# Wide early loads for the second mixture's weights, and two moves in TensorE's order

## The chip, the cores and the metric

One NeuronCore of a Trainium2 chip runs the whole program; the other cores are idle. The metric is the device time of one execution in microseconds (us), the median of a few runs. Engines are called as in the profile: PE (TensorE), PEld (its weight loads), DVE (VectorE), ACT (ScalarE), POOL (GpSimd), SP (SyncE). POOL issues the loads from memory, SP issues transposing transfers and small copies.

## The reference

Causal attention by blocks, then two mixtures that follow each other on the same tokens. All weights arrive as 64-bit floats; the tolerance lets the kernel compute with split 16-bit operands (a high and a low part, three products for one).

```python
# attention: 4 batches x 8 heads, 576 positions, 64 per head, causal by blocks of 64
scores = scale * np.matmul(q, k.transpose(0, 1, 3, 2))
scores = np.where(block_i >= block_j, scores, -1000000000.0)
attn = softmax(scores)
x = (attn @ v) laid out as 2304 tokens x 512
# first mixture
a = x @ w1            # 512 x 1024
b = x @ w2
y = (a * b @ w3) @ w_out      # 1024 x 1024, 1024 x 512
# second mixture
h = y @ w_in          # 512 x 2048
r = np.maximum(h, 0.0)
out = (r * r) @ w_out         # 2048 x 512
```

## The kernel before, in words

**Stages.** Attention runs as 16 pairs of heads (four per batch), each in three groups of rows: scores `s` on PE (L839), the largest value on DVE (L881), the exponential on ACT (L898), the probabilities `p` on ACT and DVE (L939, L946), then SP transposes `p` through a transfer (`pt`, L956) and PE multiplies it by `v` (`pv_bank`, L1031). The first mixture runs along with it, one batch behind: for each batch (576 tokens, cut into parts of 320 and 256) come the products `ab` with w1 and w2 over eight blocks f, `a` and `g` on ACT and DVE (L1277, L1284, L261), then `y` with w3 and w_out, which were multiplied together at the start (`w3o`), and the eviction `ys` on ACT (L1327) to memory. Attention is over near 375 us of the span; the first mixture's last batch and the preparation of the second mixture fill the time to some 480 us; from then to the end PE does the second mixture in blocks of 512 tokens (the first is 256). It forms `h` by a Winograd scheme with seven half-size products (`p`, L1901: operands b11, b21, t2, t3, t4, t1, b22, banks p17, p26, p45, p3), squares it, and multiplies by w_out (`p` L2069 with Strassen's scheme from the third block on, `o` L2196 before).

**Weights.** The second mixture's weights `wb` are 16 tiles of 128 x 1024 64-bit words (1 MB each), w_in in the one half of the columns and w_out in the other. `convert_pair(j)` takes tiles j and j + 8. Each half of a tile comes through `convert` (L310 to L366): a load of 128 x 512 words (512 KB) issued by POOL into one of four places `raw` (L334), two passes on ACT over the words (L342, L346), a shift and an add on DVE (L352, L355) into a place `cx`. After that the pair's norms are taken (squares on ACT L1626, L1663; small products on PE into `nq`), and ACT writes the scaled 16-bit parts `wb` (L301), DVE the low parts. Pairs 4 to 7 are kept in the four places w8_0 to w8_3 (`PAIR_HOMES`), which held w_out's words at the start of the program and are not used between the first mixture's preparation and pair 4.

**Order.** A planner (`Order`) writes every engine's instruction order. Each operation has an engine, a cost in us, the data it reads and writes, a key (rank) and a `spare`. The planner simulates the engines, and whichever engine is free next takes the lowest key among those operations whose inputs are ready by its own count; `spare` lets it count an operation's inputs as ready only that many us later, so that on PE other work comes ahead of it. An `after` entry such as ("pt", n, 2) is an order for the planner, that the operation is placed when group 2 of pair n has been transposed; it is not a wait on the chip. On the chip an engine runs its list in order and waits by semaphores for the data alone.

Of the kernel before, what the change touches and what calls it, by code (L numbers as in the profile page):

```python
# [7 lines left out]
F32 = mybir.dt.float32  # L8
# [3 lines left out]
I32 = mybir.dt.int32  # L12
# [7 lines left out]
P = 128  # L20
# [167 lines left out]
def fused_kernel(ctx: ExitStack, tc: tile.TileContext, qT, kT, vp, va, w12, w3t, wo, wb, out):  # L188
# [460 lines left out]
    def v_scales(b):  # L649
# [34 lines left out]

        key = (b * H - VSB) * HEAD
        mb_ = pv_bank[0]
        od.op(PE, 0.3, lambda: pe.matmul(mb_()[:, :P], ones(), d(), start=True, stop=True), [(ones,), (d,)], [(mb_, "pv")], key)
        e = at_buf("ve", 1, [P, H], F32, f"ve_{b}")
        t = at_buf("vsc", 2, [P, H], F32, f"vsc_{b}")
        back = at_buf("vback", 2, [P, H // 2], F32, f"vback_{b}")  # L690
# [419 lines left out]
    CHUNK = 6  # L1110
    n_unit = [0]

    def accumulate(acc, mms, n, key, c_one=c_mm, chunk=CHUNK):


        for c0 in range(0, len(mms), chunk):
            part = list(enumerate(mms))[c0 : c0 + chunk]

            def go(part=part):
                for k, (f, _) in part:  # L1120
                    l, r = f()
                    pe.matmul(acc(), l, r, start=k == 0, stop=k == len(mms) - 1)  # L1122

            keys = list(dict.fromkeys(k for _, (_, ks) in part for k in ks))
            od.op(PE, len(part) * c_one(n), go, keys, acc.keys, key)

    n_bank3 = [0]

# [24 lines left out]
    def next_key(first=K_UNIT):  # L1153
        n_unit[0] += 1
        return first + n_unit[0]
# [150 lines left out]
    def y_products(b, g, gs):  # L1306
        gt0, gn = GS[g]

        def ys_products(key=None):
            for e in range(KDM):  # L1310
                acc = Acc(gn, f"y_{b}_{g}_{e}")
                mms = []
                for f in range(KFF):
                    for a, c in PRODS:
                        mms.append((
                            lambda f=f, a=a, c=c, e=e: (w3o_view(f, a)[:, e * P : (e + 1) * P], gs[f][0][c]()),
                            [(*w3o_key(f, a), e // 2), gs[f][1][c]],
                        ))
                accumulate(acc, mms, gn, key or next_key())
                yb = buf("w2" if key else "xp", "ys", 2, [P, gn if key else GMAX], F32, f"ys_{b}_{g}_{e}")  # L1320

                def ys(yb=yb):
                    return yb()[:, :gn]

                t0 = b * S + gt0
                od.op(
                    ACT, c_act(gn), lambda acc=acc, ys=ys: act.activation(ys(), acc(), AF.Copy),  # L1327
                    [acc.key], [(yb,)], K_EVICT,
                )
                od.op(  # L1330
                    GQ, c_dma(160), lambda ys=ys, e=e, t0=t0: pool.dma_start(out=ydram[e, :, t0 : t0 + gn], in_=ys()),
                    [(yb,)], [("y", b, g, e)], K_EVICT,
                )

        if (b, g) == (B - 1, 1):
            last_y.append(ys_products)
        else:
            ys_products()
# [14 lines left out]
    KP = KFF2 // 2  # L1353
    SOON = KP // 2
    PAIR_HOMES = (0, 1, 2, 3)
    STORED_HOMES = (6, 8, 9)
    LAST = len(BLOCKS) - 1
    FIRST_S = 2
# [24 lines left out]
    def second_block():  # L1383
# [220 lines left out]
        def convert_pair(j, key):  # L1604
            if j < SOON:
                w = late(f"wbx_{j}", [P, 2, 2, 1024], f"wb_{j}", F16, 1, "wp")
            else:
                w = buf("base", f"w8_{PAIR_HOMES[j - SOON]}", 1, [P, 2, 2, 1024], F16, f"wb_{j}")
            wpair.append(w)
            home = ("wp", "cw", 4)  # L1610
            halves = {}
            for half in range(2):
                for k in range(2):
                    halves[half, k] = convert(
                        wb[j + KP * k][:, 512 * half : 512 * half + 512], None, None, None, key,
                        after=[("pt", 2 * GATE_B, 2)], home=home,
                    )
            nq, first = norms[j // SOON], SOON * (j // SOON)
            o = 2 * (j - first)
            sums = late("rs", [P, 2], f"rs_{j}", F32, 2, "wp")  # L1620
            for k in range(2):
                x, kx = halves[0, k]
                sq = buf("cv", "cx", 2, [P, 512], BF16, f"wsq_{j}_{k}")
                od.op(
                    ACT, c_act(512, 0.1),
                    lambda x=x, k=k, sq=sq: act.activation(  # L1626
                        sq(), x(), AF.Square, accum_out=sums()[:, k : k + 1]
                    ),
                    [kx], [(sq,), (sums, k)], key,
                )  # L1630

                def columns(sq=sq, k=k):
                    for kc in range(KDM):
                        pe.matmul(
                            nq()[:, o + k : o + k + 1], sq()[:, kc * P : (kc + 1) * P], ones16()[:, :1],
                            start=kc == 0, stop=kc == KDM - 1,
                        )

                od.op(PE, 0.32, columns, [(sq,), (ones16,)], [(nq, j, k)], K_NORM, S_SPARE)

            def total():
                for k in range(2):
                    pe.matmul(
                        nq()[:, 16 + o : 17 + o], ones16(), upper(sums, k, 1), start=k == 0, stop=k == 1
                    )

            od.op(PE, 0.06, total, [(ones16,), (sums, 0), (sums, 1)], [(nq, j, 2)], K_NORM, S_SPARE)
            sig = late("sig", [P, 1], f"sig_{j}", F32, 2, "wp")
            od.op(DVE, c_dve(8), lambda: shifted(th()[:, j : j + 1], nq()[:, 16 + o : 17 + o], 24), [(nq, j, 2)], [(th, j)], key)
            od.op(DVE, c_dve(8), lambda: bits(sig(), th()[:, j : j + 1], -1.0, 203.0), [(th, j)], [(sig,)], key)  # L1650
            for k in range(2):
                x, kx = halves[0, k]
                split_scaled(
                    lambda k=k: w()[:, k, 0, :512], lambda k=k: w()[:, k, 1, :512], x, 512,
                    ([(w, k, "h", 0)], [(w, k, "l", 0)], [kx]), (sig, [(sig,)]), key,
                )
            rm = late("rm", [P, 2], f"rm_{j}", F32, 2, "wp")
            for k in range(2):
                x, kx = halves[1, k]
                sq = buf("cv", "cx", 2, [P, 512], BF16, f"osq_{j}_{k}")  # L1660
                od.op(
                    ACT, c_act(512, 0.1),
                    lambda x=x, k=k, sq=sq: act.activation(  # L1663
                        sq(), x(), AF.Square, accum_out=rm()[:, k : k + 1]
                    ),
                    [kx], [(sq,), (rm, k)], key,
                )
            d = late("rd", [P, 2], f"rd_{j}", F32, 2, "wp")
            od.op(DVE, c_dve(8), lambda: shifted(rq()[:, j], rm(), 25), [(rm, 0), (rm, 1)], [(rq, j)], key)
            od.op(DVE, c_dve(8), lambda: bits(d(), rq()[:, j], -2.0, 201.0), [(rq, j)], [(d,)], key)  # L1670
            for k in range(2):
                x, kx = halves[1, k]
                split_scaled(
                    lambda k=k: w()[:, k, 0, 512:], lambda k=k: w()[:, k, 1, 512:], x, 512,
                    ([(w, k, "h", 1)], [(w, k, "l", 1)], [kx]), (lambda k=k: d()[:, k : k + 1], [(d,)]), key,
                )
# [200 lines left out]
        def h_winograd(c, j, key):  # L1877
# [12 lines left out]
            def s_of(n):  # L1890
                o, ks = sum_parts(n, j)
                return lambda a, kc: o(a)[:, kc * P : (kc + 1) * P], ks

            def product(acc, half, left, yname, spare=0.3):
                lhs, ks = left
                y = ys_[c, yname]
                mms = [(a, yn, kc) for kc in range(2) for a, yn in PRODS]

                def go():
                    for n, (a, yn, kc) in enumerate(mms):  # L1900
                        pe.matmul(  # L1901
                            acc()[:, TH * half : TH * half + TH], lhs(a, kc), y[yn]()[:, kc],
                            start=n == 0, stop=n == len(mms) - 1,
                        )

                od.op(PE, len(mms) * c_mm16(TH), go, ks + [key_of(t) for t in y], [(acc, half)], key, spare * strassen)
# [32 lines left out]
            )  # L1939
            product(b26, 0, w_of(0, 1), "b21")  # L1940
            product(b26, 1, s_of(2), "t2")
            product(b17, 1, s_of(3), "t3")
            if strassen:
                add(TH, half_of(c1, 1), half_of(b26, 1), x1, [(b26, 1), (x1,)], ck[1:])
# [2 lines left out]
            add(TH, u3, half_of(b17, 1), half_of(c1, 1), [(b17, 1), ck[1]], [(u3,)])  # L1947
            if strassen:
                add(TH, half_of(c1, 0), half_of(b26, 0), x1, [(b26, 0), (x1,)], ck[:1])
            product(b45, 0, w_of(1, 1), "t4")  # L1950
            product(b45, 1, w_of(1, 0), "t1")
            add(512, two(c2), two(b45), twice(u3), [(b45, 0), (b45, 1), (u3,)], [(c2, 0), (c2, 1)])
            add(TH, half_of(c1, 1), half_of(b45, 1), half_of(c1, 1), [(b45, 1)], [ck[1]])
# [423 lines left out]
```

## Time and profile before

| | |
|---|---|
| median of three runs | 843.76 us (842.68 to 844.37) |
| the profiled execution's own time | 844.38 us |
| its span on the page | 842.6 us (1.8 us lie around it) |
| PE busy | 822.2 us, 98% of the span |
| PEld, DVE, ACT busy | 658.6, 703.2, 606.1 us (78, 83, 72%) |
| POOL busy | 101.9 us (12%) |

The busy times say that PE is nearly always at work, and that what can be saved without removing products lies in its pauses. Matmuls overlap, so that a row's duration is longer than what it costs: one product of 256 columns in 16 bits is shown with 0.27 us but the next starts 0.11 us later, one of 320 columns 0.14 us later (a y product, 32-bit, about 0.15 us). A pause is read from starts: the distance between two successive instructions less the usual one. The idle time in square brackets behind a row is counted from the end of the row before, which is up to 0.17 us less than the pause.

### The profile page before, as it was taken

How to read it: one execution, taken by the hardware profiler on the slowest of the kernel's cores; microseconds unless marked ns; L12 is line 12 of the kernel's file. 1: busy time of each engine (PE TensorE's matmuls, PEld its weight loads, DVE VectorE, ACT ScalarE, POOL GpSimd, SP SyncE). 2: the span in 40 equal slices, each digit the busy share in tenths (PEclk: the TensorE clock that was granted, in tenths of full speed). 3: DMA queues.
4: the chain of work that ended last, by engine and by line, in shares of the span. 5: the costliest groups of instructions: out<-in, count | busy, mean ns of one | idle time of the engine just before them, and what ended most of it. 6: DMA issues, size and time to landing. Idle time of an engine off the chain costs nothing.

```text
span 842.6 us, 18679 instructions
## 1 busy us (share of the span) xinstructions
PE 822.2 (98%) x7185; PEld 658.6 (78%) x7185; DVE 703.2 (83%) x1638; ACT 606.1 (72%) x1388; POOL 101.9 (12%) x190
## 2 busy tenths in 40 slices
PE   8999999999999999999999999999999999999997
PEld 6456767778778887788879877666678888888887
DVE  6997999897778877855787889999989899787775
ACT  6997889977676777765999987565676655673552
POOL 5111211112111111011313101010020000001000
PEclk9999999999999999999999999999999999999999
DMA  8943649679998898673556422120030001001001
GB/s 325 343 147 95 195 140 213 145 167 214 203 176 171 172 180 182 145 130 104 192 179 227 140 58 69 37 90 1 2 126 1 2 7 71 1 2 51 2 1 51
DMA packets 104570, 100.18 MB, mean 119 GB/s; under 512 B 82784, under 2 KB 86624, under 8 KB 103072
## 3 DMA queue, kind: packets, MB, share of 16 engines
q0 software_dynamic: 17888, 71.18, 26.0%
q1 hardware_dynamic: 86592, 27.80, 18.5%
q8 instruction: 56, 0.92, 0.5%
q14 instruction: 34, 0.28, 0.1%
HBM read 62.78 MB, written 9.44 MB: 86 GB/s over the span
## 4 chain that ended last, share of the span: by engine, by line
PE 26%; DVE 16%; ACT 9%; issue 3%; DMA 2%; POOL 0%; DVEq 0%; ACTq 0%; POOLq 0%
PE p L1901 7%; PE p L2069 7%; PE ab L1122 6%; PE o L2196 3%; DVE c L1933 3%; ACT c L1964 2%; DMA raw<-in_wb 2%; DVE t L2024 2%; ACT c L1967 2%; PE y L1122 1%; DVE c L1975 1%; DVE gs L294 1%; DVE s L1844 1%; DVE s L1975 1%; DVE u L1933 1%
## 5 line engine op out<-in xcount | busy, mean ns | idle before, releaser
L1122 PEld LDWEIGHTS <-w 128*128 128x128 f16 x1536 | 146.9, 98 | 43.8 <-issue 6.5
L898 ACT ACTIVATE pf<-s,nm 128x192 f32<-128x192 f32 (+4 forms) x160 | 82.8, 529 | 45.2 <-DVE nm L881 44.7
L1122 PE MATMUL y<-g,w3o 128*128 128x320 f32 (+1 forms) x768 | 109.9, 299 | 1.6 <-DVE a L1284 0.8
L1122 PE MATMUL ab<-x0h,w 128*128 128x320 f16 x512 | 109.7, 299 | 0.9 <-ACT ys L1327 0.9
L1122 PEld LDWEIGHTS y<-g,w3o 128*128 128x128 f32 x768 | 103.3, 188 | 5.1 <-issue 1.2
L1122 PE MATMUL ab<-x1h,w 128*128 128x256 f16 x512 | 88.8, 273 | 0.8 <-ACT ys L1327 0.5
L2069 PEld LDWEIGHTS <-gs 128*128 128x128 f16 x816 | 79.7, 98 | 9.4 <-DVE gs L294 0.2
L1901 PEld LDWEIGHTS <-wb 128*128 128x128 f16 x768 | 75.1, 98 | 13.2 <-issue 1.2
L1122 PE MATMUL ab<-x0l,w 128*128 128x320 f16 x256 | 76.5, 299 | 0.0
L946 DVE SCALAR_TENSOR_TENSOR p<-pf,r,p 128x192 f16<-128x192 f32 (+2 forms) x120 | 62.3, 546 | 16.4 <-ACT p L939 15.8
L1122 PE MATMUL ab<-x1l,w 128*128 128x256 f16 x256 | 69.8, 272 | 0.0
L2196 PE MATMUL o<-wb,g 128*128 128x512 f16 x288 | 67.1, 379 | 0.0
L939 ACT ACTIVATE p<-pf,r 128x192 f16<-128x192 f32 (+2 forms) x120 | 61.2, 558 | 6.6 <-issue 2.6
L1901 PEld LDWEIGHTS <-st 128*128 128x128 f16 x576 | 56.1, 98 | 9.3 <-issue 2.2
L2069 PE MATMUL p<-ts,gs 128*128 128x256 f16 x480 | 61.1, 273 | 0.0
L1964 ACT ACTIVATE c<-c,beta 128x512 f32<-128x512 f32 x48 | 34.3, 715 | 35.3 <-DVE c L1933 35.1
L839 PE MATMUL s<-kraw,qraw 64*128 64x288 f32 (+4 forms) x384 | 54.0, 408 | 0.1
L2196 PEld LDWEIGHTS <-g 128*128 128x128 f16 x288 | 28.0, 98 | 28.9 <-issue 0.4
L839 PEld LDWEIGHTS s<-kraw,qraw 64*128 64x128 f32 x384 | 33.9, 186 | 15.0 <-issue 8.5
L292 ACT ACTIVATE gs<-c 128x512 f16<-128x512 f32 (+1 forms) x56 | 30.0, 536 | 21.1 <-DVE c L1975 20.9
L2069 PE MATMUL p<-wb,gs 128*128 128x256 f16 x336 | 44.5, 273 | 0.0
L873 DVE TENSOR_REDUCE nm<-s 128x2 f32<-128x384 f32 (+1 forms) x64 | 42.2, 686 | 1.0
(268 smaller groups left out, 1943.9 us busy)
## 6 DMA issues: line engine op xcount, KB each, us to landing
raw<-in_wb POOLq DMA_DIRECT2D x32, 512.0 KB, 4.9
raw<-in_w3t POOLq DMA_DIRECT2D x8, 1024.0 KB, 10.1
raw<-in_w POOLq DMA_DIRECT2D x16, 512.0 KB, 4.6
yraw<-ydram POOLq DMA_DIRECT2D x12, 512.0 KB, 4.6
vraw<-in_vp POOLq DMA_DIRECT2D x16, 320.0 KB, 4.7
qraw<-in_qT POOLq DMA_DIRECT2D x16, 288.0 KB, 4.3
kraw<-in_kT POOLq DMA_DIRECT2D x16, 288.0 KB, 4.9
vmix<-v SPq DMA_DIRECT2D x24, 160.0 KB, 4.5
```

What stands on the lines that cost most here:

```text
L292: od.op(ACT, c_act(n), lambda: act.activation(hi(), src(), AF.Copy), ks, kh, key)
L839: pe.matmul(o[:, h] if t == 4 else o, q()[rows, q_start(t) : q_start(t) + 128], keys_()[rows, c], start=True, stop=True,)
L873: lambda k=k, t=t, nm=nm, banks=banks: dve.tensor_reduce(out=nm()[:, k], in_=banks[0]()[:, :, S_COL[t] : S_COL[t] + n_keys(t)], op=ALU.max ...
L898: act.activation(o, view(a, t), AF.Exp, bias=nm()[:, k, a : a + 1], scale=SCALE, accum_out=ssum()[:, k, a : a + 1],)
L939: lambda o=o, nk=nk, a=a, k=k, w=weights, p16=p16, r=r: act.activation(p16()[:, o : o + nk], w(a, k), AF.Copy, scale=r()[:, k, a : a + 1]),
L946: lambda o=o, nk=nk, a=a, k=k, w=weights, p16=p16, r=r: dve.scalar_tensor_tensor(out=p16()[:, o + nk : o + 2 * nk], in0=w(a, k), scalar=r( ...
L1122: pe.matmul(acc(), l, r, start=k == 0, stop=k == len(mms) - 1)
L1901: pe.matmul(acc()[:, TH * half : TH * half + TH], lhs(a, kc), y[yn]()[:, kc], start=n == 0, stop=n == len(mms) - 1,)
L1933: DVE, c_dve(n), lambda: dve.tensor_tensor(out=o(), in0=x(), in1=y(), op=ALU.add), r, w, K_OUT
L1964: lambda src=src, k=k: act.activation(src(), src(), AF.Relu, scale=beta()[:, j, k : k + 1]),
L2069: pe.matmul(acc()[:, TH * u : TH * u + TH], t()[:, o : o + P], r(b), start=first and n == 0 and u == tiles[0], stop=last and n == 2 and u ...
L2196: pe.matmul(o(), g[gx]()[:, cols], wt(f)[:, a, 512:1024], start=(begin and n == 0), stop=(last and n == 2),)
```

## The change

Three things are changed. (1) For pairs j = 0 and 1 of the second mixture's weights the four tiles are loaded whole, 128 x 1024 words each, into the places w8_0 to w8_3, and ACT's two passes go over a whole tile at a time; DVE's shift and add are still done by halves. The planner's gate for them is group 2 of pair 13 (`GATE_W`), while that of the half loads is later, in the last batch. (2) In the second mixture's products `h_winograd` the product of t4 (P4, first half of bank p45) is written ahead of the product of t3 (P7, second half of bank p17). (3) The planner counts `spare` 0.8 for the y products, and 1.2 for the small product with `vdiag` (L687), which carries the scale of the next batch's v to all partitions.

```diff
@@ v_scales
-        od.op(PE, 0.3, lambda: pe.matmul(mb_()[:, :P], ones(), d(), start=True, stop=True), [(ones,), (d,)], [(mb_, "pv")], key)
+        od.op(PE, 0.3, lambda: pe.matmul(mb_()[:, :P], ones(), d(), start=True, stop=True), [(ones,), (d,)], [(mb_, "pv")], key, 1.2)
...
-    def accumulate(acc, mms, n, key, c_one=c_mm, chunk=CHUNK):
+    def accumulate(acc, mms, n, key, c_one=c_mm, chunk=CHUNK, spare=0.0):
...
-            od.op(PE, len(part) * c_one(n), go, keys, acc.keys, key)
+            od.op(PE, len(part) * c_one(n), go, keys, acc.keys, key, spare)
@@ y_products
-                accumulate(acc, mms, gn, key or next_key())
+                accumulate(acc, mms, gn, key or next_key(), spare=0.8)
...
+    WIDE_HOMES = {0: (0, 1), 1: (2, 3)}
+    GATE_W = 26
@@ convert_pair
+            if j in WIDE_HOMES:
+                words = []
                 for k in range(2):
...
+                    raw = buf("base", f"w8_{WIDE_HOMES[j][k]}", 1, [P, 1024], I64, f"raw_{n_raw[0]}")
+                    ku, kw = (raw, "u"), (raw, "l")
+                    od.op(
+                        GQ, c_dma(1024), lambda raw=raw, k=k: pool.dma_start(out=raw(), in_=wb[j + KP * k]),
+                        [("pt", GATE_W, 2)], [ku, kw], key,
                     )
...
+                    od.op(ACT, c_act(1024, 0.04), scale_up, [], [ku], key)
+                    od.op(
+                        ACT, c_act(1024, 0.04),
+                        lambda word=word: act.activation(word(0), word(0).bitcast(U32), AF.Copy, scale=2.0**-29),
+                        [], [kw], key,
+                    )
...
+            else:
+                for half in range(2):
+                    for k in range(2):
+                        halves[half, k] = convert(
...
@@ h_winograd
             product(b26, 1, s_of(2), "t2")
+            product(b45, 0, w_of(1, 1), "t4")
             product(b17, 1, s_of(3), "t3")
...
-            product(b45, 0, w_of(1, 1), "t4")
             product(b45, 1, w_of(1, 0), "t1")
```

**POOL near 327 us.** The rows are POOL's transfers around the first two reloads of y (`yraw`) for the second mixture. Before:

```order
L643 DMA kraw_4857<-in_kT 128x576
L1331 DMA ydram<-ys_1_3_4865 128x256
L1471 DMA yraw_31_4945<-ydram 128x2x256
L1471 DMA yraw_32_5246<-ydram 128x2x256
L1331 DMA ydram<-ys_0_0_5498 128x320
L334 DMA raw_5560<-in_wb 128x512
L1331 DMA ydram<-ys_0_1_5606 128x320
L1331 DMA ydram<-ys_0_2_5647 128x320
L1331 DMA ydram<-ys_0_3_5677 128x320
```

After, in the same place:

```order
L643 DMA kraw_4849<-in_kT 128x576
L1331 DMA ydram<-ys_1_3_4860 128x256
L1473 DMA yraw_31_4928<-ydram 128x2x256
L1621 DMA raw_5085<-in_wb 128x1024
L1621 DMA raw_5113<-in_wb 128x1024
L1621 DMA raw_5125<-in_wb 128x1024
L1621 DMA raw_5134<-in_wb 128x1024
L1473 DMA yraw_32_5237<-ydram 128x2x256
L1331 DMA ydram<-ys_0_0_5472 128x320
```

The four whole tiles stand between the first and the second reload of y; before, the first load of `wb` stood behind both and behind an eviction of y of the last batch.

**PE at the second `vdiag`.** The rows are PE's in the first y products of the second batch's first part; `y_0_1` is one accumulator, x6 are six products. Before:

```order
L1122 MATMUL y_0_1_2539<-g_0_0_1496,w3o_509 128x320 x6
L1122 MATMUL y_0_1_2539<-g_0_0_1496,w3o_744 128x320 x6
L687 MATMUL pv_bank<-vdiag_2429,ones 128x128 [waits DVE_49]
L1122 MATMUL y_0_1_2539<-g_0_4_1933,w3o_971 128x320 x6
L1122 MATMUL y_0_1_2539<-g_0_4_1933,w3o_1231 128x320 x6
```

After:

```order
L1122 MATMUL y_0_1_2539<-g_0_0_1490,w3o_509 128x320 x6
L1122 MATMUL y_0_1_2539<-g_0_0_1490,w3o_744 128x320 x6
L1122 MATMUL y_0_1_2539<-g_0_4_1933,w3o_971 128x320 x6
L687 MATMUL pv_bank<-vdiag_2429,ones 128x128 [waits DVE_49]
L1122 MATMUL y_0_1_2539<-g_0_4_1933,w3o_1231 128x320 x6
```

One more group of six y products stands ahead of the `vdiag` product.

**PE in a step of the second mixture.** The rows are one of the Winograd steps (third block, second column pair): the end of the t2 products (bank p26), and what follows. Before:

```order
L1901 LDWEIGHTS st_7449
L1901 MATMUL p_2_1_9028<-t2h_8834,st_7449 128x256
L1901 LDWEIGHTS st_7669
L1901 MATMUL p_2_1_9020<-t3h_8889,st_7669 128x256 [waits Activation_49]
L1901 LDWEIGHTS st_7669
L1901 MATMUL p_2_1_9020<-t3l_8925,st_7669 128x256
```

After:

```order
L1949 LDWEIGHTS st_7476
L1949 MATMUL p_2_1_9018<-t2h_8819,st_7476 128x256
L1949 LDWEIGHTS wb_6273
L1949 MATMUL p_2_1_9037<-t4h_8891,wb_6273 128x256 [waits DVE_49]
L1949 LDWEIGHTS wb_6273
L1949 MATMUL p_2_1_9037<-t4l_8898,wb_6273 128x256
```

Behind t2's last product stand now the six of t4 (into p45, with a converted weight `wb`), and t3's (into p17, with a sum of weights `st`) come behind them; before it was the other way round.

## Rows read from the trace of the kernel before

**Rows 1.** PE around 185 to 188 us, timeline: start, duration, instruction, idle before.

```profile
185.01 2.03 PE L1122 MATMUL y<-g,w3o 128*128 128x320 f32 x12
188.03 0.49 PE L687 MATMUL pv_bank<-vdiag,ones 128*128 128x128 f32 x2 [0.99 <-DVE x1l L1047]
```

**Rows 2.** What PE waited for in the whole span: total, times, longest (us).

```profile
PE ab L1122 <- ACT ys L1327: 1.5, 3, 0.7
...
PE p L1901 <- ACT x L1938: 0.8, 3, 0.3
...
PE y L1122 <- ACT g L261: 0.5, 1, 0.5
```

**Rows 3.** Windows of 20 us: length, busy PE, PEld, DVE, ACT, POOL; PEclk, DMA share, GB/s.

```profile
120.00:140.00 20.00, 18.82 (x152) 14.45 (x150) 19.52 (x58) 18.06 (x46) 3.77 (x7) 1.00 0.82 187
320.00:340.00 20.00, 20.00 (x190) 14.68 (x187) 15.78 (x40) 14.39 (x42) 3.63 (x6) 1.00 0.84 169
400.00:420.00 20.00, 19.07 (x162) 17.07 (x161) 14.37 (x34) 18.02 (x41) 6.33 (x11) 1.00 0.59 196
420.00:440.00 20.00, 20.00 (x165) 14.54 (x164) 16.74 (x37) 20.00 (x46) 3.74 (x7) 1.00 0.55 170
500.00:520.00 20.00, 20.00 (x155) 16.46 (x155) 20.00 (x51) 12.87 (x27) 3.66 (x6) 1.00 0.24 79
```

**Rows 4.** ACT timeline in 400 to 460 us, the two waits for a transfer.

```profile
413.25 0.67 ACT L342 ACTIVATE raw<-raw 128x512 f32<-128x512 f32 x1 [1.85 <-DMA raw<-in_wb]
...
456.26 0.67 ACT L342 ACTIVATE raw<-raw 128x512 f32<-128x512 f32 x1 [0.70 <-DMA raw<-in_wb]
```

**Rows 5.** PE timeline at 418 us, the instruction after the pause.

```profile
418.47 0.30 PE L1122 MATMUL ab<-x0h,w 128*128 128x320 f16 x1 [0.69 <-ACT ys L1327]
```

**Rows 6.** ACT instruction groups by form: busy us, mean ns, idle before.

```profile
L342 ACT ACTIVATE raw<-raw 128x512 f32<-128x512 f32 x48 | 32.4, 675 | 3.3 <-DMA raw<-in_wb 3.3
...
L342 ACT ACTIVATE raw<-raw 128x1024 f32<-128x1024 f32 x5 | 5.7, 1145 | 0.0
```

**Rows 7.** PE timeline of two Strassen steps, the second and third product.

```profile
662.03 0.27 PE L1901 MATMUL p<-t2h,st 128*128 128x256 f16 x1
662.62 0.27 PE L1901 MATMUL p<-t3h,st 128*128 128x256 f16 x1 [0.32 <-ACT x L1938]
...
663.27 0.27 PE L1901 MATMUL p<-t4h,wb 128*128 128x256 f16 x1
...
670.37 0.27 PE L1901 MATMUL p<-t2h,st 128*128 128x256 f16 x1
670.70 0.27 PE L1901 MATMUL p<-t3h,st 128*128 128x256 f16 x1
```

**Rows 8.** DVE timeline before 659 us, the last reads of the step's banks.

```profile
657.88 0.94 DVE L1933 TENSOR_TENSOR c<-p,c 128x256 f32<-128x256 f32 x2
```

**Rows 9.** POOL timeline at 327 to 330 us.

```profile
327.56 0.71 POOL L1471 DMA_DIRECT2D yraw<-ydram  x1
```

**Rows 10.** Transposes issued in 326 to 333 us, and their time to landing.

```profile
L956 SPq DMA_TRANSPOSE pt<-p x3: 1232/1407/1786, 329.2 to 332.5; - x3
...
DMA to landing us min/median/max: 5.0/5.0/6.0
```

**Rows 11.** The same for 341 to 349 us.

```profile
DMA to landing us min/median/max: 3.1/3.2/3.4
```

**Rows 12.** The same for 120 to 150 us.

```profile
DMA to landing us min/median/max: 3.4/7.1/8.4
```

**Rows 13.** PE timeline at 340 us, the first product of the next pair.

```profile
340.38 0.52 PE L1031 MATMUL pv_bank<-pt,v 128*64 128x256 f16 x8
```

**Rows 14.** Page, part 6: transfers, KB each, median us from issue to landing.

```profile
raw<-in_wb POOLq DMA_DIRECT2D x32, 512.0 KB, 4.9
raw<-in_w3t POOLq DMA_DIRECT2D x8, 1024.0 KB, 10.1
```

**Rows 15.** Page, part 2: bytes moved in 40 slices of 21 us.

```profile
GB/s 325 343 147 95 195 140 213 145 167 214 203 176 171 172 180 182 145 130 104 192 179 227 140 58 69 37 90 1 2 126 1 2 7 71 1 2 51 2 1 51
```

More of the change, by code (lines that the diff above doesn't have):

```diff
@@ L1611, in convert_pair, with word, scale_up @@
             halves = {}
-            for half in range(2):
+            if j in WIDE_HOMES:
+                words = []
                 for k in range(2):
-                    halves[half, k] = convert(
-                        wb[j + KP * k][:, 512 * half : 512 * half + 512], None, None, None, key,
-                        after=[("pt", 2 * GATE_B, 2)], home=home,
-                    )
+                    n_raw[0] += 1
+                    raw = buf("base", f"w8_{WIDE_HOMES[j][k]}", 1, [P, 1024], I64, f"raw_{n_raw[0]}")
[3 more added lines that the diff above has]
+                        [("pt", GATE_W, 2)], [ku, kw], key,
+                    )
+                    def word(m, cols=slice(0, 1024), raw=raw):
+                        return raw().bitcast(I32).rearrange("p (n two) -> p n two", two=2)[:, cols, m]
+                    def scale_up(word=word):
+                        up = word(1).bitcast(F32)
+                        act.activation(up, up, AF.Prelu, scale=2.0**-112, alpha=2.0**32)
+                    od.op(ACT, c_act(1024, 0.04), scale_up, [], [ku], key)
[4 more added lines that the diff above has]
+                    )
+                    words.append((word, ku, kw))
+                for half in range(2):
+                    cols = slice(512 * half, 512 * half + 512)
+                    for k, (word, ku, kw) in enumerate(words):
+                        n_raw[0] += 1
+                        x = buf(*home, [P, 512], I32, f"cx_{n_raw[0]}")
+                        od.op(
+                            DVE, c_dve(256),
+                            lambda x=x, word=word, cols=cols: dve.tensor_scalar(
+                                out=x(), in0=word(1, cols), scalar1=3, scalar2=None, op0=ALU.logical_shift_left
+                            ),
+                            [ku], [(x,)], key,
+                        )
+                        od.op(
+                            DVE, c_dve(512),
+                            lambda x=x, word=word, cols=cols: dve.tensor_tensor(
+                                out=x(), in0=x(), in1=word(0, cols), op=ALU.add
+                            ),
+                            [kw], [(x,)], key,
+                        )
+                        halves[half, k] = (lambda x=x: x().bitcast(F32)), (x,)
+            else:
+                for half in range(2):
+                    for k in range(2):
+                        halves[half, k] = convert(
+                            wb[j + KP * k][:, 512 * half : 512 * half + 512], None, None, None, key,
+                            after=[("pt", 2 * GATE_B, 2)], home=home,
+                        )
```

## Prediction

> **What bounds the kernel now.** PE. The page's busy times come first (the table above): 98% for PE. The windows of 20 us then show where it isn't at work: in most stretches PE has 20.00 of 20 us, in 400 to 420 us 19.07, in 120 to 140 us 18.82, with PEclk 1.00 throughout, the higher level, 2.4 GHz [rows 3]. The list of PE's waits tells what ended the pauses [rows 2], and the timeline of each place tells what stood behind. The removed idle time counts as time saved only if nothing else of the same place is late next. The number of PE's products is the same before and after, so the sum consists of pauses alone.
>
> **The change part by part.** I count against the profiled execution's 844.38 us, which lies 0.62 us above the median of 843.76 us; the sum is then taken from the median.
>
> *1. The vdiag product later.* At 185.01 us twelve y products take 2.03 us on the page; less the last one's overhang of some 0.39 us, eleven steps are 0.15 us each [rows 1]. So the vdiag product could start at 185.01 + 12 x 0.15 = 186.8 us and starts at 188.03: a pause of 1.2 us, released by DVE [rows 1]. After the change six more y products stand ahead of it, 6 x 0.15 = 0.9 us. **-0.9.** The third vdiag product did not pause, and the first sits in a stretch where DVE has 19.52 of 20 us [rows 3]: what PE would not wait there it would wait at the next product that needs DVE, so it counts nothing.
>
> *2. Spare for y.* Where y starts before ACT has given the last g, PE waits 0.5 us in one place [rows 2]. There a group of six products of the next accumulator, 0.9 us, now goes between. **-0.6**, the idle time and about 0.1 us of what the overlap hides.
>
> *3. P4 ahead of P7.* t3's product writes the second half of bank p17, and so must wait until ACT has copied the first half away (`x`, L1938). At 662.03 us the last t2 product starts, and t3's follows at 662.62 instead of 0.11 us later: a pause of 0.48 us, of which 0.32 are listed as idle [rows 7]. So each listed wait costs some 0.16 us more than its idle time. The list has three such waits, 0.8 us together [rows 2], which is 0.8 + 3 x 0.16 = 1.3 us. There are shorter ones below the list's limit, as at 670.37, where the distance to 670.70 is 0.22 us too long [rows 7]; I take three of them, 0.6 us. Six products take 0.65 us (t3's from 662.62 to 663.27 [rows 7]), more than any of these pauses; t4's six now stand in them. t4 needs its bank p45, last read by DVE in the step before; these reads end at 658.8 us (657.88 + 0.94), over 3 us ahead [rows 8]. What comes due next: DVE's sum u of t3's bank, now 0.65 us later, still has t1's products ahead of the sum that needs both. **-1.8** (0 to -1.9).
>
> *4. What ACT and the transfers hold up in the last batch.* Three times PE waits for ACT's eviction of y ahead of an `ab` product, 1.5 us in all [rows 2], the longest at 418.47 us [rows 5]. Why is ACT late? It has 18.02 us of work in 400 to 420 and 20.00 of 20 in 420 to 440 [rows 3], and before that it had stood still 1.85 us for a half load of `wb` at 413.25, and again 0.70 us at 456.26 [rows 4]. The four whole tiles take eight half loads out of this stretch, with 8 x 2 ACT passes of 0.675 us [rows 6]. **-2.0** (1.5 + 3 x 0.16, bounds 0 and -2.4).
>
> *5. Where this work goes.* Eight wide ACT passes of 1.145 us each [rows 6], 9.2 us, now stand in attention's last part, between some 337 and 352 us; before, ACT had 14.39 us of work in 320 to 340 [rows 3]. The planner spreads the pairs around them, but an estimate from the durations of before, laid along the new order, gives some 26 us of ACT's work against 28 of PE's for the stretch from the third block f to the first y. That is tight: ACT at 92%. In 400 to 420 us, with 90%, PE lost 0.9 us [rows 3]. **+0.5** (0 to 1.5).
>
> *6. The loads and the transposes.* This is the unknown. POOL issues the first yraw load at 327.56 us [rows 9], and the four whole tiles now stand right behind it. Their places are not in use, the gate is the planner's alone and no wait on the chip, so they start at once. They bring 4.2 MB. Right behind, at 329.2 us, SP issues the first two transposes of pair 13's next group; in the kernel before they land 5.0 to 6.0 us later [rows 10] and are needed at 340.38 us [rows 13]. So they have some 10 us before PE waits. How long do 4.2 MB occupy the transfer engines? At 325 to 343 GB/s, the two highest slices of the page [rows 15], 12 to 13 us; by the whole w3 tiles, eight of which land 10.1 us after issue when several are under way [rows 14], about 10. From 328.5 us on, with some 2 us until the first bytes move, that ends between 340 and 343. The transfers have 0.84 of their time taken in 320 to 340 already [rows 3]. If the transposes share and end with the loads, PE waits from 340.4 to some 343: **+2.6**, bounds 0 and +5.5. The lower bound is the landing time of transposes under load in 120 to 150 us, 7.1 us in the middle and 8.4 at most, against 3.2 undisturbed [rows 12, 11]; there the loads were of 512 KB and less, a half as much at once. I take the upper middle since four whole tiles in a row are nowhere in the trace while transposes run.
>
> The Trainium skill, "DMA: Bandwidth & Descriptors", section "Queues, rings and completion order", says that each transfer engine takes turns between its queues, packet by packet. By that rule a transpose would get its turn between the loads' packets, and term 6 would come nearer to 0; the trace agrees as far as transposes do land under load, later but within 8.4 us [rows 12].
>
> *Sum:* -0.9 - 0.6 - 1.8 - 2.0 + 0.5 + 2.6 = **-2.2 us**; from the median, 843.76 - 2.2 = 841.6 us (842.2 against the profiled execution).
>
> **The rivals.**
> *A, the transposes are not held.* Landing 8.4 us after 329.2 to 330.5 us gives 338.9 at most, ahead of 340.38 [rows 12, 13]. Then term 6 is 0: -4.8 us, 839.0. For it: the rows under load. Against it: those loads were smaller.
> *B, slower.* The loads, queued in one row, hold up all of pair 13: its transposes, and behind them the copies of v and the next group's transposes, which SP issues in order. The gains without terms 5 and 6 are 5.3 us; from a hold of 7 us on (transposes landing later than about 347 us), with ACT's 0.5 us, the change loses by more than the measurement can tell. That takes transfers that share the 4.2 MB's time at the 169 GB/s of this stretch [rows 3], which makes 25 us of them. A hold of 8 us would give 843.76 - 5.3 + 0.5 + 8 = 847. Against it: the stretch's rate is low because little is asked for.
> *C, the gains come back as other pauses.* In 500 to 520 us DVE has 20.00 of 20 us [rows 3]; if that stretch is DVE's, what PE wins ahead of it (terms 1, 2, 4: 3.5 us) is waited out there, and only term 3 remains, against terms 5 and 6: 843.76 - 1.8 + 3.1 = 845.1, or 842.5 without the hold. Middle: 843.8, no change. Against it: PE has 20.00 there too, so DVE's work is not yet late.
> *D, the tiles don't relieve ACT.* With half of the conversions gone the planner draws other work of the last pairs forward, ACT stays full, and the waits of term 4 stay: 843.6 with the hold, about the same as before.
>
> **How the numbers follow.** The forecast (hold of some 0.5 to 5 us, other terms as counted) has 0.42, 839.5 to 844; A 0.22, near 839; B 0.13, near 847; C 0.14, near 843.8; D 0.09, near 843.6. A measurement of this kernel can tell about 0.2%, 1.7 us, from no change: faster is below 842.1, slower above 845.4. Faster: about 0.27 of the forecast's 0.42, all of A, 0.05 of C and D: 0.55. Slower: B and 0.04 of C: 0.17. The same: 0.28. The range leaves out a little of A's low end and most of B: 838.3 to 846.0.
>
> **What would show it.** In the profile of the changed kernel: transposes issued near 328 us landing 10 us or more later, and a wait of PE for `pt` ahead of the first products near 339 us (term 6; none there is A); no wait of ACT for `raw` and none of PE for `ys` near 413 to 418 and 456 to 461 us (term 4); no wait for `x` of L1938 (term 3); the second vdiag product with a pause of at most 0.3 us (term 1). The prediction is wrong if pair 13 waits over 5 us, if DVE's waits in 500 to 570 us grow by what was won ahead of them, or if ACT's wide passes make pauses for attention near 340 to 360 us.

## The result and the profile after

The change makes the kernel slower: a median of 850.0 us (847.6 to 854.6, 20 runs) against 843.35 us (20 runs), a ratio of 1.0079 with an interval of 1.0064 to 1.0095. The profiled execution took 850.0 us with a span of 848.2; before it was 844.38 and 842.6. So 5.6 us have to be found in the span. Two executions, those of spread_d below at 860.0 and 862.4 us, count as slow and are left out of its ratio.

The loss is in one place, and it is larger than 5.6 us, since gains elsewhere offset a part of it. The waits of PE over the whole span, as in [rows 2], total, times and longest:

```profile
PE pv_bank L1031 <- DMA pt<-p: 7.3, 2, 6.5
...
PE pv_bank L374 <- DVE wsum L423: 2.9, 3, 1.4
...
PE ab L1122 <- ACT a L1277: 0.2, 1, 0.2
```

The waits of [rows 2] for ACT's `ys`, `x` and `g` are gone, and a new one stands on top: PE waits 7.3 us for transposes. Its place, in PE's timeline from 338 us on:

```profile
338.18 0.39 PE L1031 MATMUL pv_bank<-pt,vmix 128*64 128x128 f16 x8
345.10 0.21 PE L1031 MATMUL pv_bank<-pt,vmix 128*64 128x64 f16 x1 [6.53 <-DMA pt<-p]
346.05 0.27 PE L1031 MATMUL pv_bank<-pt,vmix 128*64 128x64 f16 x3 [0.74 <-DMA pt<-p]
346.25 0.45 PE L1122 MATMUL ab<-x0h,w 128*128 128x320 f16 x1
346.49 0.47 PE L1122 MATMUL ab<-x0l,w 128*128 128x320 f16 x1
349.95 0.43 PE L1122 MATMUL ab<-x0h,w 128*128 128x320 f16 x2
350.23 0.30 PE L1122 MATMUL ab<-x0l,w 128*128 128x320 f16 x1
```

Pair 13's products, which follow each other without a gap at 340.38 us in [rows 13], stop after 20 of 24. PE stands still from about 338.5 to 346.1 us, but for one product at 345.10: 6.53 + 0.74 us of idle time, about 7.6 us by the starts. Behind it the `ab` products start 0.27 us apart instead of 0.14 (346.25 to 349.95 us, 14 products, 3.7 us for what needs 1.9). The window shows why (length, busy PE, PEld, DVE, ACT, POOL; PEclk, DMA share, GB/s):

```profile
330.00:340.00 10.00, 8.57 (x78) 5.99 (x75) 5.62 (x15) 2.83 (x10) 0.72 (x1) 1.00 1.03 354
340.00:350.00 10.00, 4.16 (x19) 2.40 (x19) 2.78 (x7) 4.84 (x16) 0.00 (x0) 0.66 1.22 207
350.00:360.00 10.00, 10.00 (x111) 6.66 (x110) 7.52 (x21) 6.99 (x17) 0.00 (x0) 1.00 0.63 119
```

PEclk is 0.66 in 340 to 350 us. By single microseconds it is 1.00 until 343 us, 0.56 from 343 to 344, 0.50 from 344 to 349 and 1.00 again from 350 on: it falls while PE stands still, and the products from 346.25 us on run at the lower of TensorE's two levels, 1.2 GHz, until 2.4 GHz is back at about 350. That is another 1.8 us, 9.4 with the standstill.

Now SP, which issues the transposes: start, time of the issue itself.

```profile
326.48 1.28 SPq L956 DMA_TRANSPOSE pt<-p  x1
327.87 13.72 SPq L956 DMA_TRANSPOSE pt<-p  x1
...
341.69 4.55 SPq L956 DMA_TRANSPOSE pt<-p  x2
```

The landing of the transposes issued in 326 to 348 us, as in [rows 10] to [rows 12]:

```profile
DMA to landing us min/median/max: 3.5/12.0/18.6
```

and of the four whole tiles, which POOL issues from 326.4 us on:

```profile
DMA to landing us min/median/max: 8.4/12.8/15.9
```

The two transposes that the stopped products need are issued at 326.48 and 327.87 us. The first lands 18.6 us later, at 345.1, just when PE goes on; the second lets go the last three products at 346.05. In the kernel before they landed after 5.0 to 6.0 us [rows 10]. The loads land after 8.4 to 15.9 us, the last of them at 344.0. SP is held as well: the second transpose's issue takes 13.72 us, where those of this stretch took 1.2 to 2.0 us in the kernel before, and the next two are issued only from 341.69 us on (two in 4.55 us). PE needs those at 351.8 us and didn't wait for them.

What the transfer engines did meanwhile is in the queues' packets of the ten us from 330 to 340 (packets, MB, share of 16 engines; q0 carries POOL's loads, q1 SP's transposes and copies), first the changed kernel:

```profile
q0 software_dynamic: 465, 3.40, 95.1%
q1 hardware_dynamic: 467, 0.12, 7.2%
```

then the same stretch of the changed kernel without its wide loads (experiment no_wide, below):

```profile
q1 hardware_dynamic: 4624, 1.59, 94.9%
q0 software_dynamic: 81, 0.26, 7.7%
```

With the loads in flight 465 of their packets passed and 467 of the other queue: one for one. This holds by single microseconds too: from 332 to 340 us the counts are 48 and 48, 47 and 47, 55 and 56, 18 and 17, 47 and 47, 55 and 55, 55 and 55, 52 and 52. The loads' packets brought 3.40 MB, the transposes' 0.12 MB (some 256 bytes each). Without the loads 4624 packets of that queue passed in the same time, 4129 of them under 512 bytes, with four transposes issued: some thousand small packets for each. So the reading is: the queues take turns by packets, and each small packet of a transpose waits for a large one of the loads. The held issue on SP cannot be the cause for the first transpose, whose own issue took 1.28 us and which landed late all the same. The experiments test the reading.

### The profile page after: what moved, and what is told of

Read it like the earlier page. It is cut to its first block, busy times and chain, and to the rows that moved or that the text cites. A ratio compares the mean times of both kernels' runs of the same rounds, so it can differ in the third digit from the quotient of the medians.

```text
span 848.2 us, 18651 instructions
## 1 busy us (share of the span) xinstructions
PE 824.1 (97%) x7185; PEld 658.9 (78%) x7185; DVE 701.9 (83%) x1638; ACT 604.2 (71%) x1380; POOL 100.3 (12%) x186
## 4 chain that ended last, share of the span: by engine, by line
PE 43%; DVE 9%; ACT 5%; issue 1%; DVEq 0%; ACTq 0%
PE p L1949 14%; PE p L2117 11%; PE ab L1122 7%; PE o L2244 5%; PE y L1122 5%; DVE t L2072 1%; DVE c L1981 1%; ACT c L2012 1%; DVE s L1892 1%; ACT c L2015 1%; DVE g L294 1%; PE pv_bank L1031 1%; DVE ts L2094 1%; DVE gs L294 1%; DVE c L2023 0%
## 6 DMA issues: line engine op xcount, KB each, us to landing
raw<-in_w3t POOLq DMA_DIRECT2D x8, 1024.0 KB, 10.1
```

## The experiments

All kernels are cut from the changed one; "before" is measured anew on the same chip in each group of runs. PE's order around pair 13's products is the same in the changed kernel, no_wide, one_pair, spare_only and late30.

### Without the wide loads

```diff
-    WIDE_HOMES = {0: (0, 1), 1: (2, 3)}
+    WIDE_HOMES = {}
```

> The changed kernel without its wide loads (all tiles as half loads at the old gate): P4 ahead of P7 and the two spares alone. The order of PE around pair 13's products at 338 us is the same as in the changed kernel. Theory (the four loads hold up pair 13's transposes): no wait for pt there, PEclk 1.00, and the pauses at 415 to 461 us for ACT (2.4 us) are back; the vdiag, y and x pauses stay away: 843.4 - 0.9 - 0.9 - 1.8 = about 840 us. Rival 1 (the new order around pair 13, made by the spares, issues its transposes too near their use): the wait of some 7 us at 338 us stays and the time is about 848 to 852.

Measured: 840.45 us against 844.12, ratio 0.995 (0.9924 to 0.9976). No wait for `pt`, PEclk 1.00. The profiled spans of the changed kernel and of this one, 848.2 and 838.7 us, differ by 9.5 us, which the standstill and the lower clock (9.4) account for. So the loads are the loss, and the order around pair 13 is not (rival 1 falls). One expectation failed: the pauses at 415 to 461 us did not come back. The window of 400 to 420 us in no_wide:

```profile
400.00:420.00 20.00, 20.00 (x174) 17.95 (x172) 15.44 (x33) 20.00 (x47) 7.19 (x13) 1.00 0.70 219
```

and in the changed kernel:

```profile
400.00:420.00 20.00, 20.00 (x222) 18.71 (x221) 16.92 (x40) 14.61 (x34) 4.31 (x10) 1.00 0.29 94
```

In no_wide ACT is as full as it can be, 20.00 of 20 us, and PE still doesn't wait. In the changed kernel the wide loads took 5.4 us of ACT's work away from here, and PE has the same 20.00. In [rows 3] it had 19.07. So these pauses go without the tiles.

### One pair instead of two

```diff
-    WIDE_HOMES = {0: (0, 1), 1: (2, 3)}
+    WIDE_HOMES = {0: (0, 1)}
```

> Wide loads for pair 0 alone (two tiles, 2.1 MB instead of 4.2 MB), in the same place of POOL's order; PE's order around pair 13 unchanged. Theory (transposes and loads take turns until the loads are through): the second transpose's issue on SP takes some 6 to 7 us instead of 13.7, the hold at pair 13 falls from 7.6 us to 0 to 1.5, TensorE's clock stays 1.00, and the time is 840 to 842. Rival 1 (order): about 850 as in the changed kernel. Rival 2 (any wide load behind yraw blocks SP for a fixed time): hold over 5 us, 847 or more.

Measured: 843.57 us, ratio 1.0002 (0.9987 to 1.0016); 1.5 us above what was expected, with the hold as expected. SP's second issue:

```profile
327.58 6.74 SPq L956 DMA_TRANSPOSE pt<-p  x1
```

the landing of the transposes issued in 326 to 348 us (min, median, max):

```profile
DMA to landing us min/median/max: 3.1/3.5/11.9
```

and PE's wait:

```profile
PE pv_bank L1031 <- DMA pt<-p: 0.8, 1, 0.8
```

The longest landing is 11.9 us with 2.1 MB, 18.6 with 4.2 MB, and 6.4 with none (no_wide); SP's second issue takes 6.74, 13.72 and 1.78 us. Both grow with the loads. The 11 to 12 us from issue to use cover the smaller one but for 0.8 us. Rival 2, a fixed time, falls. Of the rest of the 3 us above no_wide, PE's waits for ACT ahead of scores (`s`, 0.7 us in two places) are new in this trace; what remains was not followed up.

### The same tiles with half the row

```diff
-                        GQ, c_dma(1024), lambda raw=raw, k=k: pool.dma_start(out=raw(), in_=wb[j + KP * k]),
+                        GQ, c_dma(1024), lambda raw=raw, k=k: [pool.dma_start(out=raw()[:, c : c + 512], in_=wb[j + KP * k][:, c : c + 512]) for c in (0, 512)],
```

> The changed kernel with each of the four tiles loaded by two transfers of 512 words per row (4 KB rows instead of 8 KB) in the same place; the same 4.2 MB, ACT's passes still over whole tiles. Theory (queues take turns packet by packet, so that a transpose's 256 B packet waits for one load packet): smaller load packets give the transposes about twice as many turns, SP's second issue takes 7 to 9 us, the hold falls to 2 to 4 us, and the time to 843 to 846. Rival 3 (the bytes alone count: the transposes end when 4.2 MB are through, whatever the packets): hold 7 us, about 850 as in the changed kernel.

Measured: 857.57 us, ratio 1.016 (1.0136 to 1.0185). Neither was right: it got worse by some 7 us (ratio 1.016 against 1.0079). PE's wait:

```profile
PE pv_bank L1031 <- DMA pt<-p: 14.4, 2, 11.0
```

the landing of the loads:

```profile
DMA to landing us min/median/max: 6.9/16.7/18.5
```

and the packets of 330 to 340 us:

```profile
q0 software_dynamic: 394, 1.42, 78.7%
q1 hardware_dynamic: 929, 0.24, 27.3%
```

PE waits 14.4 us, 7.1 more than in the changed kernel. Of the loads only 1.42 MB passed between 330 and 340 us, against 3.40 in the changed kernel. I had reckoned that the loads' end would stay where it was and the transposes get more turns before it; they did get more packets through (929 against 467), but the loads lost more than half of their rate, and the meeting lasted longer. Over ten us 394 to 929 is not one for one, yet by single microseconds the counts are nearly equal from 336 to 343 us, as in the last of them:

```profile
q0 software_dynamic: 88, 0.33, 92.8%
q1 hardware_dynamic: 87, 0.02, 9.5%
```

That is also more turns than in the changed kernel, where from 330 to 341 us 43 to 62 of the loads' packets passed in a microsecond, but for one of 18. What spoils it is the stretch from 333 to 338 us, in which the loads' queue passed only 8 to 25 packets in each. POOL issued the eight loads over 7.2 us there (327.7 to 334.9), with pauses, and the four of the changed kernel in 1.7 (326.4 to 328.1). Why so few passed is not known. That the bytes alone count is refuted as well.

### Half rows where no transposes are

```diff
-    GATE_W = 26
+    GATE_W = 30
```

together with the edit of rows4k.

> rows4k (each tile by two transfers of 4 KB rows) at gate 30, behind the last pair's transposes. If the 8 us that rows4k lost against the changed kernel come from more packets meeting the transposes, there is no loss here: no wait for pt, the loads land in 12 us or less, 841 to 843 as late30. If half rows are slow by themselves, the loads land in 16 us or more here too, and ACT or PE waits for them near 380 to 400 us.

Measured: 842.73 us, ratio 0.9997 (0.998 to 1.0013). The loads of 370 to 410 us landed so:

```profile
DMA to landing us min/median/max: 3.9/7.5/10.9
```

At most 10.9 us, against 18.5 with transposes in flight: half rows are not slow by themselves, and the loss comes with meeting the transposes. Why 4 KB rows lose so much more of their rate in that meeting than 8 KB rows, the runs don't tell.

### Four tiles in a row, behind attention

The edit of the gate (26 to 30) alone.

> The changed kernel with gate 30 in place of 26: the same four wide loads in a row, but behind attention's last pair, where no transposes are issued any more. Theory (the loss is the meeting of loads and transposes): no wait for pt over 0.3 us, clock 1.00, 840 to 841, as without wide loads, since the ACT pauses are gone there already. Rival (the four loads in a row, or ACT's wide passes, cost something by themselves wherever they are): 843 or more.

Measured: 842.06 us, ratio 0.9968 (0.9944 to 0.9992). No wait for `pt`, PEclk 1.00 in 340 to 350 us. The same four wide loads in a row and the same wide passes of ACT cost no hold where they meet no transposes. It is some 1.6 us above no_wide; in the trace a new pause of PE ahead of a norm's small product (listed as 0.68 us of idle time at 450.68 us) accounts for some 0.7 of them.

### The tiles one by one

```diff
-    GATE_W = 26
+    GATE_W = (20, 22, 24, 26)
...
-                        [("pt", GATE_W, 2)], [ku, kw], key,
+                        [("pt", GATE_W[2 * j + k], 2)], [ku, kw], key,
```

> The four wide loads apart from each other: one each with pairs 10, 11, 12 and 13 (gates 20, 22, 24, 26 in place of 26 for all). Theory: each load of 1 MB delays the transposes near it by some 3 us, which the distance from issue to use (some 10 us) covers; no wait of PE for pt over 0.5 us, clock 1.00, the ACT pauses at 415 to 461 us stay away as in the changed kernel: 843.4 - 0.9 - 0.9 - 1.8 - 2.4 + 0.5 = about 838 us. Rival 4 (a whole tile near transposes costs a wait wherever it is): four waits of 1 to 2 us, 842 to 846.

Measured: 840.87 us, ratio 0.9965 (0.9953 to 0.9977). The transposes land late here too, PE doesn't wait for them:

```profile
L956 SPq DMA_TRANSPOSE pt<-p x7: 1250/3168/4411, 324.8 to 347.5; - x7
...
DMA to landing us min/median/max: 4.1/8.1/13.3
```

The window where the changed kernel stood still:

```profile
340.00:350.00 10.00, 10.00 (x91) 6.93 (x90) 6.43 (x16) 7.10 (x21) 0.00 (x0) 1.00 1.28 167
```

An issue on SP takes up to 4.41 us and a landing up to 13.3, but the distance from issue to use covers it; PE has 10.00 of 10 us where it lost 5.8 in the changed kernel. That distance is not the same here: the planner's order differs, and the two transposes beside the last tile, issued at 330.48 and 332.62 us, land at 343.8 and 345.0 and are used from 346.19 us on, 14 to 16 us after their issue instead of 11 to 12. So smaller delays and more room came together, and with 1.2 us to spare the run does not tell them apart. It is not faster than no_wide: no gain of the conversions done early is seen once the spares are in. The 838 us expected counted a gain of ACT's that was no longer there.

With gates (14, 16, 18, 20), earlier by three pairs:

> The changed kernel with the four wide loads apart and earlier: one each with pairs 7, 8, 9 and 10 (gates 14, 16, 18, 20). Theory: as spread_b, no wait for pt over 0.5 us, 840 to 841, and no gain over no_wide since the ACT pauses they were to remove are gone by the spare for y. Rival (early tiles give ACT room that is worth something): 839 or less.

Measured: a median of 845.11 us over all ten executions, which lie between 839.2 and 862.4; ratio 1.0005 (0.9972 to 1.0038). The best executions are as no_wide; in the profiled one (846.39) PE waits 1.5 us for transposes in a pair's products near 295 us, and 1.2 and 0.3 us for ACT behind it. So here a tile beside each of four pairs did cost a wait. The rival (early tiles are worth something) gets no support; what scatters so much was not settled.

### The parts alone

The wide loads alone (kernel before, edit 1 only):

> The kernel before with the wide loads of four tiles at gate 26 and nothing else. Theory (the loads alone hold pair 13): a wait for pt of 6 to 9 us near 340 us, TensorE's clock at the lower level for some us behind it, second issue of SP about 13 us; ACT's pauses at 415 to 461 us gone (-2.4): 844.1 + 7.6 + 1.9 - 2.4 = 851. Rival 1 (only together with the new order of the spares): no such wait, 842.

Measured: 849.74 us against 844.06, ratio 1.0057 (1.0034 to 1.008). PE's waits:

```profile
PE pv_bank L1031 <- DMA pt<-p: 5.0, 2, 4.2
...
PE ab L1122 <- ACT ys L1327: 0.5, 1, 0.5
```

the window of the hold:

```profile
340.00:350.00 10.00, 4.97 (x42) 3.15 (x37) 3.44 (x8) 5.07 (x16) 0.00 (x0) 0.83 1.11 266
```

and the packets ahead of it:

```profile
q0 software_dynamic: 499, 3.49, 96.7%
q1 hardware_dynamic: 319, 0.08, 4.4%
```

The hold is there without the spares: 5.0 us of waiting, PEclk 0.83, 319 packets of the transposes' queue against 499 of the loads. They are fewer because the first of them pass only behind 332 us; from then on it is one for one again, as from 339 to 340 us:

```profile
q0 software_dynamic: 61, 0.39, 94.7%
q1 hardware_dynamic: 61, 0.02, 6.9%
```

And of the waits for `ys`, 1.5 us in [rows 2], 0.5 remain. That fits the expectation that the tiles end a part of them, but p4_only, without tiles, keeps no more.

P4 ahead of P7 alone:

> The kernel before with P4 ahead of P7 and nothing else. Theory: the six pauses ahead of t3's products (2.0 us) go, the pauses at 415 to 461 us (ACT) and at the second vdiag stay: 844.1 - 1.9 = 842.2. Rival: DVE, which is late in 500 to 570 us, gives half of it back elsewhere: 843.2.

Measured: 842.95 us, ratio 0.9984 (0.9951 to 1.0018). In its trace the waits for `x` are gone, and of the three for `ys` one stays (0.5 us, the row is shown below); by the time alone theory and rival can't be told apart, nor P4 from no change.

The spares alone:

> The kernel before with the two spares for y and vdiag and nothing else. Since without wide loads the ACT pauses at 415 to 461 us were gone as well, the theory now is that the spare for y removes them, by placing y's groups so that ACT's evictions are not awaited: vdiag -0.9, y -0.9, ACT -2.4, against 0.9 us of a new wait at 171 us and 0.4 ahead of it: about -2.9, 841. Rival (P4's move shifts the last batch and removes them): the pauses at 415 to 461 us stay, 842.5.

Measured: 841.65 us, ratio 0.9973 (0.9945 to 1.0). PE's waits in p4_only:

```profile
PE pv_bank L687 <- DVE x1l L1047: 1.0, 1, 1.0
...
PE ab L1122 <- ACT ys L1327: 0.5, 1, 0.5
```

and in spare_only:

```profile
PE pv_bank L374 <- DVE wsum L423: 2.8, 3, 1.4
PE pv_bank L1031 <- DMA pt<-p: 2.8, 1, 2.8
...
PE p L1949 <- ACT x L1986: 0.5, 2, 0.2
```

With the spares alone no wait for `ys` or at the second vdiag is left, only that for `x`, which is P4's. So the two spares end the pauses at 415 to 461 us without tiles and without P4: in this trace y products run on (from 414.98 and from 456.77 us) where PE waited for an eviction. The execution profiled here (847.44 us) also had a wait of 2.8 us for transposes, at 222.5 us, where loads of v stand in the same place; so such a hold came without the wide loads too.

The spare for y and P4, without that for vdiag:

> P4 ahead of P7 and the spare for y alone; no spare for vdiag, no wide loads. Theory (term 1: the vdiag spare is worth 0.9 us at the second vdiag product and nothing at the first): some 0.9 us more than no_wide, 841.4. Rival (what the vdiag spare saves is paid back at the sums near 127 us and in a new wait near 279 us): 840.5 as no_wide.

Measured: 842.1 us, ratio 0.999 (0.9968 to 1.0013), 1.6 us above no_wide5, with intervals that overlap. That speaks for the theory and does not decide it. In the traces PE is idle 0.98 us in 180 to 200 us here and 0.10 in no_wide, which is the vdiag spare's 0.9. But there is a second difference:

```profile
PE ab L1122 <- ACT ys L1327: 0.8, 2, 0.5
```

With P4 and the spare for y a wait of 0.54 us for `ys` at 459.14 us is still there, as in the kernel before at 461.12. So the spare for y alone does not end all of these pauses, and p4_only lacks two of them without any spare. Both spares together leave none (no_wide, spare_only); which edit ends which pause is not settled.

### The faster version

P4 and both spares without the wide loads (no_wide), measured once more:

> The kernel of no_wide once more, in five rounds: P4 ahead of P7 and both spares, no wide loads. Expected as before, 840.5 against 844 (ratio 0.995); were the first measurement luck, the ratio would be 0.997 to 1.0 as for the single parts.

Measured: 840.49 us against 843.16, ratio 0.9961 (0.9941 to 0.9981). It is faster than both given kernels; spread_b (0.9965) can't be told from it.

## Why the prediction was wrong

It forecast 841.6 us, faster; the kernel is slower. First the changed kernel's rows at the second vdiag product, then the steps one by one:

```profile
185.77 1.78 PE L1122 MATMUL y<-g,w3o 128*128 128x320 f32 x11
187.66 0.49 PE L687 MATMUL pv_bank<-vdiag,ones 128*128 128x128 f32 x2
```

- **Term 1**, vdiag, -0.9: right. By these rows vdiag could start at 185.77 + 11 x 0.15 = 187.4 us and starts some 0.25 us later, instead of 1.2. What the first vdiag product saved was indeed lost at the next sum that needs DVE: the row for `wsum` stands at 2.9 us, in the trace of before at 2.5.
- **Term 2**, y, -0.6: right; the wait for `g` is gone. Together with the vdiag spare it did more than this term gave it (term 4).
- **Term 3**, P4, -1.8: the row for `x` is gone, as forecast. Alone P4 measured 1.1 us (ratio 0.9984, 0.9951 to 1.0018), an interval that holds the 1.8 us and also no gain at all.
- **Term 4**, ACT, -2.0: the gain came, its cause was wrong. I traced PE's pauses back to ACT's load and that to the transfers, and took the removal of ACT's load as what ends them. But PE's pauses also end when something else stands in PE's order there, and edit 3, the spares, put it there: no_wide keeps ACT at 20.00 of 20 and has no pauses. Tiles and spares together earn this once.
- **Term 5**, ACT's wide passes, +0.5: about 0; PE waits 0.2 us for ACT's `a`. The passes stand from 358.58 us on, behind the hold, and not between 337 and 352, so the tight stretch that this term feared did not come about.
- **Term 6**, the loads and the transposes, +2.6, bounds 0 and +5.5: this step failed. It measured 7.6 us of hold and 1.8 us at the lower clock, 9.4 together. PE came to need the transposes some 12 us after the first load's issue (326.4 to 338.5), as forecast (328.5 to 340.4). Three things were mis-sized. The loads took longer: I let them end at most 14.5 us after that moment (328.5 to 343), and the last landed after 17.6 (326.4 to 344.0). Their rate was as reckoned, 3.40 MB in ten us, but of the 5.2 MB that passed on their queue from 326 us on some 0.7 MB were of loads issued before them (5.2 less 4.2 for the tiles and 0.3 for the reload of y behind them). I let the transposes end with the loads, while they get a packet for a packet: up to 341 us, where the loads' packets thin out, some 570 of theirs had passed, and the two landed at 345.1 and 346.0, up to 2.0 us behind the last load. These 3.1 and 2.0 us are what the hold of 2.6 lacked. And I counted no clock behind the hold. My lower bound, 8.4 us under load, came from loads of 512 KB and less, a half as much at once, and was no bound for four whole tiles in a row. The 10.1 us of the w3 tiles [rows 14] are a median over eight loads, of which four were issued close together (13.67 to 17.78 us) and the others alone, so they are not the time of four in a row. No run shows the 2 us until the first bytes move: in the kernel before, POOL's first load is issued at 1.29 us and bytes move from 2.65 us on.

The Trainium skill's rule in "DMA: Bandwidth & Descriptors", section "Queues, rings and completion order", that an engine takes turns by packets, agrees with the trace as far as the counts go: 465 against 467. I read it the wrong way round. Here a turn of the transposes was worth 256 bytes and a turn of the loads some 7.3 KB (3.40 MB in 465 packets), so that turns by packets did not protect the transposes: 0.12 MB passed in ten us, for as long as the loads lasted.

**Rival B** named the mechanism (pair 13's transposes held, 847 us) and its condition, a hold of 7 us or more. It got 0.13, with a price from the low rate of that stretch, which is not what happened: the loads moved 3.40 MB in ten us, 340 GB/s. **D** falls: ACT was relieved (14.61 of 20 us in 400 to 420). **C** falls: PE's idle time in the windows of 20 us from 500 to 580 adds up to 0.6 us in the kernel before and in the changed one. But terms 1 to 4 add up to 5.3 us, and without the loads the kernel gained 3.7 and 2.7 us by its two measurements (3.9 by the profiled span). So a part of the gains was not seen. PE's waits in no_wide for `wsum` (0.4 us more) and for ACT's `a` (0.9 us against 0.3) are some of it; the rest is open.

## What to carry to other kernels

Ask of a load that is moved early not only whether its place is free and its bytes fit, but which transfers of small packets are in flight beside it and who waits for the next ones on the issuing queue: four loads in a row cost 9 us here. One beside each of the pairs 10 to 13 cost nothing that was seen, in an order that also left the transposes more time, and one beside each of the pairs 7 to 10 still a wait of 1.5 us. If two edits each could end the same pause, credit it once, and test them apart. And when a load's gate lies only in the planner's order, read from the trace when the issuing engine really gets to it: POOL issued these loads as soon as the one ahead of them was issued.

## What the runs showed of the hardware

- Loads and transposes in flight together passed packet for packet (465 and 467 in 10 us, and 43 to 61 of each in most single microseconds of the changed kernel and of wide_only), 3.40 MB against 0.12 MB. A transpose's issue then occupied SP for 13.72 us; without the wide loads (no_wide) it took 1.2 to 2.6 us in this stretch.
- TensorE's granted clock fell to the lower level while PE stood still (0.56 from 343 to 344 us, after the last product but one near 338.5) and stayed there for some 3.7 us of products, which cost 1.8 us on top.
- Loads in 4 KB rows moved less beside transposes than loads in 8 KB rows: 1.42 MB against 3.40 MB in the same ten us; apart from transposes they landed in 10.9 us at most.
